# First two attention units gathered whole, and the means of v copied out of PSUM once

## The chip, the cores and the metric

The kernel runs on one core of one Trainium2 chip. The metric is the device time of one execution in microseconds: 601.21 us is the median of three runs of the kernel before (601.02 to 601.26).

## The reference, cut to what matters

Attention with a local window and block summaries, then two MLPs with their own activations. Shapes: 2 batches, 8 heads, 768 positions, head size 64; 1536 tokens of 512 in the MLPs, 2048 hidden.

```python
k_sum = k.reshape(B, H, nb, 32, D).max(axis=3)        # nb = 24
v_sum = v.reshape(B, H, nb, 32, D).mean(axis=3)
scores_l = scale * q @ k^T, where |i - j| < 16, else -1e9
scores_s = scale * q @ k_sum^T + log(32)
a = softmax(concat(scores_l, scores_s))
x = a @ concat(v, v_sum)                               # heads side by side: 1536 x 512
h = x @ w_in1;  P = a0 + a1 h + a2 h^2 + a3 h^3;  Q = 1 + |b0||h| + |b1| h^2
x = (P / (Q + 1e-6)) @ w_out1
h = x @ w_in2;  out = (h * cos(h)) @ w_out2
```

## The kernel before

The weights come as 64 bit floats. DVE puts each block together as 32 bit from its two halves (`f<-raw`, three instructions, L760 to L768), and it is then split into a high and a low part (`w`), so that a product is three matmuls of the fast 32 bit kind. Per block of 128 hidden units and 512 tokens there is a stage `h` (12 matmuls, L864), an elementwise chain (`te`, `tu`, `tf`, then `gh` and `gl`), and a stage `acc` (12 matmuls, L1106) that adds into four PSUM banks `acc0` to `acc3`. The second MLP takes its hidden blocks in pairs with seven products instead of eight (L962).

Attention has 12 units of 128 queries. A unit turns q round (`qtp`, copied to `qT`), gathers for each half of 64 queries the 96 keys of its window and the 24 block maxima into `kw` (a part of the tile `room`), and forms the scores of even and odd heads in two banks (`sp`, L626). Then come 8 score steps: DVE adds the mask and takes the maximum (`sc`, `mn`, L656), and ACT does exp with its sum (`su`, L660). The probabilities are scaled, transposed (`ptp`, copied to `pt`) and multiplied with `vw` (`avp`, L734). `vw` is one of four tiles: 96 rows of v by a load from DRAM (L722), and 24 rows of v's block means. The output goes split into `xH` and `xL`, which the first `h` reads.

At the start k of batch 0 comes in 8 loads (a pair of heads and half the positions each, into `part`), is transposed on PE into early banks (`ktp`, L463), copied to `big` and reduced to block maxima (L471). Two loads of q serve units 0 and 1. v of batch 0 comes in three loads; two positions are added (L514), and three matmuls make the means in one bank, `vmp` (L517).

The order is written out. The program first lists 3040 operations, each with its possible engines; a table (`ORDER`) then gives for every place which operation is issued next and on which engine. Each engine keeps that order, and so does SP, which issues nearly all DMAs. Waits follow from the data.

The change touches, in `v_mean0`, the copies of the means (L521 to L526); in `q_tile`, units 0 and 1 (L565 to L575); in `attn_a`, the gathering by pairs of heads (`gather`, L608 to L645); in `add_a`, where the first q is listed; and the table. At the end, `mlp_end` (L1138) does the last accumulator in two halves of 256 columns: matmuls of half one, its copy by ACT, matmuls of half two, its copy by DVE, each half with its own output DMA.

Of the kernel before, what the change touches and what calls it, by code (L numbers as in the profile page):

```python
# [11 lines left out]
F32 = mybir.dt.float32  # L12
# [9 lines left out]
QC = 1.0 + 1e-6  # L22
# [13 lines left out]
for _p, _t in (("AA", .143), ("AP", .17), ("AT", .25), ("AV", .14), ("PA", .08), ("PP", .08), ("PT", .15),  # L36
# [20 lines left out]
    "c-rk)ON?g6RsQOA-*w;jf4}<g{`)o4-P7Zq=^1+-9?wi>?7=wWB#vccTP8ROa%>aJ1|csTD`5dy#8QX>i%1qqK!CD{;t"  # L57
    "+(8B3OY4Qp5_0B|FwE*dTFk)xEbTSwz6PtN-r*KB~^+JKs5{sv+FasgQC63MdEQF^-Fy3?2?-dffr`rQ~1-$In5*agKK"
    "P57-&k`|Y{do&Zb5F~_gT=?vlcRZ+5_?~j0?E?gY!IH~l<s?;B1UKL`F0`eH%5ZANt0$7PXEnM*sR~{H}mI<6w-*>?BU"
    "w4xwmORI7%gcCzc#wUS>jW~_#U#^V`a~lC>24UnzonvA;c_U3vv1$SRovaZeVJXy^`Cy~^7auPd1?!nzJ6uv@y&<NZ+`"  # L60
    "8Mw>ED=A3eIk&ttiDaG*BVw$I@F;>PaIx39muxxd(Y=ffW@HdYHP=iglW=6rGZjrshU!{-h@eK^1J)ZxJ;>_7368{+8j"
    ";MSXm&dxp_+y1F~VQ}RqJI|~Bz0Y2LM!ga|T|Iqw?QV7VBG$@s?fO*Ct8sCCRP10l$glL5`LcI>+{@=xKAj$y<^JJ442"
    "v6sb9=~xtzMO2RSc6Kt}pU9E@x@~;ZeNX8$zF1@9S!JQQShgm`$%0FJ5&gSr!hCqgxkK#9{Hc#z7R^O2XaUca;9zPVn+"
    "p^l0R7JpZRF1n$~7S3bSkd}@AX-`(4t&1Ro~bL%Z^+<cSYxcBykb1fFvL>3L>FGhL%imPtCER!-(;%xSs*cCfa{A(X<d"
    "g8s5_j%-%-1A5L?PpzGI68Qv;K_hXeaHXH@@B+^P~KIcxqE>hE%+By@KrAu&v@`c>GHvEMcR8f{LCf~qoI10$!O&sF4<"
    "IUs)<-%jThqm#g6mLXzPn?_B;HQ1^=%R=d2j@er2!s8J4|G4El1h`^K5#e2&%n{=aR;>)6(d|JYjm%PQWO|2q~5J|7(c"
    "!GA7334h=*jEZvb&&U;IMnrlfj=_n}=lu!?z>~Lg=Mkh^Th7g^|A0qVa3X=r9J2rsyud+NIS#x?UI>q3In*8iAG^qyix"
    "ohc_#rr4?9#L!QvwP64RLw?SHQ;~<KrLb+xY%1Y=18VR)3D_&)6s3?@(qqA2|ysJ-ZDV4j_VlZ4)x2xEx22tOu`p%)3!"
# [1258 lines left out]
```

## Time and profile before

| | |
|---|---|
| median of three runs | 601.21 us (601.02 to 601.26) |
| the profiled execution | 601.26 us, of which the trace spans 599.4 |
| PE busy | 585.9 us (98%) |
| DVE busy | 548.4 us (92%) |
| ACT, POOL busy | 434.1 us (72%), 304.3 us (51%) |
| granted PE clock | full in all 40 slices |

The profile has one row of times for each engine. PE's share of 98% counts modelled ends of pipelined matmuls, so short gaps don't show in it. Where PE is not the last to be waited for is at the start, in the first 100 us, where attention and the first blocks of the MLP run side by side, and in the last few us.

### The profile page before, as it was taken

What the parts mean: (1) busy time and instruction counts of PE and PEld (TensorE: products, weight loads), DVE (VectorE), ACT (ScalarE), POOL (GpSimd) and SP (SyncE); (2) the same over time, 40 slices, a digit from 0 to 9 for tenths busy, and PEclk for the clock granted to TensorE, in tenths of its full rate; (3) what the DMA queues carried; (4) which work ended last, traced back from release to release, by engine and by line L of the source; (5) the groups of instructions that cost most, each with busy time, mean ns of one, the idle gap of its engine ahead of it and who ended that gap; (6) DMA issues with size and microseconds to landing.
All of it is one profiled execution on the core that took longest, in us unless ns stands there. A gap on an engine that the chain in (4) does not pass through costs nothing.

```text
span 599.4 us, 10933 instructions
## 1 busy us (share of the span) xinstructions
PE 585.9 (98%) x3897; PEld 501.0 (84%) x3897; DVE 548.4 (92%) x1119; ACT 434.1 (72%) x954; POOL 304.3 (51%) x303
## 2 busy tenths in 40 slices
PE   8879999999999999999999999999999999999997
PEld 7568878888888888888888888888989989998996
DVE  4999999979999999998999999999999998887874
ACT  3989999877587756876789897766767566554653
POOL 5587975247537564557577542444355423732130
PEclk9999999999999999999999999999999999999999
DMA  9897874200321313311220112123322331100104
GB/s 264 218 258 192 204 209 120 75 0 2 106 71 37 106 36 105 106 52 56 70 71 1 36 36 71 37 71 104 109 71 70 106 108 36 35 1 1 53 1 158
DMA packets 68862, 51.85 MB, mean 87 GB/s; under 512 B 37304, under 2 KB 63160, under 8 KB 68808
## 3 DMA queue, kind: packets, MB, share of 16 engines
q1 hardware_dynamic: 68664, 51.03, 29.0%
q8 instruction: 30, 0.49, 0.3%
q14 instruction: 24, 0.20, 0.1%
q10 hardware_dynamic: 144, 0.13, 0.1%
HBM read 47.71 MB, written 3.15 MB: 85 GB/s over the span
## 4 chain that ended last, share of the span: by engine, by line
PE 87%; DVE 9%; ACT 2%; DMA 1%; issue 0%; POOL 0%; SPq 0%; POOLq 0%; DVEq 0%; ACTq 0%
PE acc L1106 43%; PE h L864 22%; PE h L962 18%; DVE sc L656 2%; DMA vw<-in_v_dram 1%; PE avp L734 1%; DVE f L764 1%; DVE f L768 1%; PE ptp L687 1%; PE sp L626 1%; PE warm L356 1%; PE ktp L463 1%; DVE f L760 1%; PE vmp L542 0%; DVE big L471 0%
## 5 line engine op out<-in xcount | busy, mean ns | idle before, releaser
L1106 PE MATMUL acc<-gh,w 128*128 128x512 f32 (+1 forms) x416 | 123.1, 378 | 0.0
L1106 PE MATMUL acc<-w,gh 128*128 128x512 f32 x382 | 119.3, 394 | 0.0
L864 PE MATMUL h<-xH,w 128*128 128x512 f32 (+1 forms) x320 | 99.1, 371 | 0.1
L777 POOL TENSOR_TENSOR gl<-te,gh 128x512 fp32r<-128x512 f32 (+1 forms) x48 | 62.7, 1307 | 67.2 <-ACT gh L322 33.5
L1106 PEld LDWEIGHTS acc<-gh,w 128*128 128x128 f32 x416 | 75.3, 188 | 14.9 <-issue 1.5
L1106 PE MATMUL acc<-gl,w 128*128 128x512 f32 (+1 forms) x208 | 77.6, 373 | 0.0
L1106 PEld LDWEIGHTS acc<-w,gh 128*128 128x128 f32 x382 | 66.7, 189 | 9.4
L1106 PE MATMUL acc<-w,gl 128*128 128x512 f32 x191 | 74.3, 389 | 0.0
L1023 POOL TENSOR_TENSOR tu<-tu,tf 128x512 f32<-128x512 f32 (+1 forms) x41 | 51.4, 1255 | 41.2 <-ACT tf L1015 40.9
L777 POOL TENSOR_TENSOR w<-f,w 128x512 fp32r<-128x512 f32 x39 | 54.4, 1397 | 29.5 <-ACT w L322 15.0
L864 PEld LDWEIGHTS h<-xH,w 128*128 128x128 f32 x320 | 58.5, 188 | 10.6 <-DVE big L495 0.3
L864 PE MATMUL h<-xL,w 128*128 128x512 f32 (+1 forms) x160 | 58.9, 368 | 0.0
L864 PE MATMUL h<-big,w 128*128 128x512 f32 x216 | 52.0, 389 | 0.0
L768 DVE SCALAR_TENSOR_TENSOR f<-raw,f 128x512 int32<-128x512 int32 x64 | 48.3, 759 | 0.3
L1013 ACT ACTIVATE tu<-h,co 128x512 f32<-128x512 f32 (+1 forms) x52 | 33.9, 652 | 19.3 <-PE h L864 18.2
L764 DVE SCALAR_TENSOR_TENSOR f<-raw,f 128x512 int32<-128x512 int32 x64 | 47.3, 745 | 0.6
L864 PEld LDWEIGHTS h<-big,w 128*128 128x128 f32 x216 | 40.6, 188 | 8.4
L1106 PEld LDWEIGHTS acc<-gl,w 128*128 128x128 f32 x208 | 39.1, 188 | 7.0
L1106 PEld LDWEIGHTS acc<-w,gl 128*128 128x128 f32 x191 | 35.9, 188 | 7.9
L1057 ACT ACTIVATE tu<-te 128x512 int32<-128x512 f32 x27 | 17.1, 632 | 32.5 <-DVE te L987 32.2
L324 POOL TENSOR_SCALAR w<-f 128x512 fp32r<-128x512 f32 x28 | 20.0, 715 | 39.8 <-DVE f L768 35.1
L1033 ACT ACTIVATE h<-tf 128x512 f32<-128x512 f32 (+1 forms) x52 | 29.6, 570 | 12.0 <-DVE te L1027 10.8
(222 smaller groups left out, 1530.9 us busy)
## 6 DMA issues: line engine op xcount, KB each, us to landing
raw<-in_moe_w_in_dram SPq DMA_DIRECT2D x32, 512.0 KB, 4.6
raw<-in_moe_w_out_dram SPq DMA_DIRECT2D x32, 512.0 KB, 3.4
vw<-in_v_dram SPq DMA_DIRECT2D x24, 192.0 KB, 3.5
qk<-in_q_dram SPq DMA_DIRECT2D x10, 256.0 KB, 5.3
out_dram<-part SPq DMA_DIRECT2D x8, 256.0 KB, 2.8
part<-in_k_dram SPq DMA_DIRECT2D x8, 192.0 KB, 4.8
big<-in_v_dram SPq DMA_DIRECT2D x3, 512.0 KB, 6.7
qk<-in_k_dram SPq DMA_DIRECT2D x6, 256.0 KB, 5.4
```

The lines of the kernel that those rows point to most:

```text
L324: nc.gpsimd.tensor_scalar(out=o, in0=i, scalar1=1.0, scalar2=1.0, op0=ALU.mult, op1=ALU.mult)
L656: lambda e, pr=pr, hh=hh, sv=sv, sp=sp: nc.vector.tensor_tensor_reduce(out=sv()[:, pr, :], in0=sp.t[:, pr, :], in1=m.t, op0=ALU.add, op1=A ...
L764: lambda e: nc.vector.scalar_tensor_tensor(out=ft.t.bitcast(I32), in0=lohi()[1], scalar=-0x40000000, in1=ft.t.bitcast(I32), op0=ALU.bitwis ...
L768: lambda e: nc.vector.scalar_tensor_tensor(out=ft.t.bitcast(I32), in0=lohi()[0], scalar=29, in1=ft.t.bitcast(I32), op0=ALU.logical_shift_r ...
L777: lambda e: E[e].tensor_tensor(out=lo(), in0=x(), in1=hi().bitcast(F32), op=ALU.subtract),
L864: nc.tensor.matmul(out=h.t[:, 0:n], lhsT=lt, rhs=rt[:, kk, cs], start=(k0 == 0 and i == 0), stop=(k0 == 2 and i == 5))
L962: nc.tensor.matmul(out=bank.t[:, c], lhsT=lt, rhs=rt, start=start and i == 0, stop=stop and i == 5, skip_group_check=True)
L1013: lambda e: nc.scalar.activation(out=U(), in_=H(), func=ACTF.Square, scale=b1s))
L1023: lambda e: E[e].tensor_tensor(out=U(), in0=U(), in1=Z(), op=ALU.add))
L1033: lambda e: nc.scalar.activation(out=H(), in_=Z(), func=ACTF.Exp, scale=-1.0))
L1057: lambda e: nc.scalar.activation(out=K().bitcast(I32), in_=S_(), func=ACTF.Identity, scale=1.0 / (2.0 * math.pi)))
L1106: nc.tensor.matmul(out=dst, lhsT=lt, rhs=rt, start=(un.start and not have and i == 0), stop=(un.stop and i == 2), skip_group_check=have)
```

## The change

1. `v_mean0`: only the first `vw` tile gets the means from PSUM by an engine's copy. The other three get them from that tile by loads inside SBUF. Before, two were copied, and two loaded.
2. `q_tile` for units 0 and 1: the transposes of all four pairs of heads are one operation, and one copy of 512 columns takes the place of two of 256.
3. `attn_a` for units 0 and 1: the maxima, the windows and the score matmuls are gathered for all four pairs at once, as the other units have it; before, pair by pair.
4. `add_a`: q of unit 0 is listed after all pairs of k, not after the first.
5. A new table for 3018 operations, in place of 3040. Engines change all through the program.

```diff
 ORDER = (
-    "c-rk)ON?g6RsQOA-*w;jf4}<g{`)o4-P7Zq=^1+-9?wi>?7=wWB#vccTP8ROa%>aJ1|csTD`5dy#8QX>i%1qqK!CD{;t"
...
+    "c-rk)TaRQ{bzXa|z0dtt=Tdd5s_WWaeV^{089cXk&)CMygv{6&JYbANu%p-zWXBkgfM7uqq{twF5(^>{*)K>4cp?TOBS"
...
-        for i in range(2):
+        for i in range(1):
             P.op([("A", act(512, True)), ("V", dve(512))], [], [vp, vws[i]["m"]],
                  lambda e, i=i: cp(e, vws[i].t[WK:KW], vp.t[WK:KW]))
-        for vw in vws[2:]:
+        for vw in vws[1:]:
             P.op([("S", 0.2)], [vws[0]["m"]], [vw["m"]],
                  lambda e, vw=vw: nc.sync.dma_start(out=vw.t[WK:KW], in_=vws[0].t[WK:KW]))
...
+        if u < 2:
+            raws = [x for x, _ in q_first]
+
+            def tr(e):
+                for pr in range(NP):
+                    h0 = 2 * (pr % 2)
+                    transpose_pairs(tp.t[:, pr, :], q_first[pr // 2][1]()[:, h0:h0 + 2], 64 * u, 64)
...
-        if u < 2:
-            for i in range(2):
-                def tr(e, i=i):
-                    for x in range(2):
-                        transpose_pairs(tp.t[:, 2 * i + x, :], q_first[i][1]()[:, 2 * x:2 * x + 2], 64 * u, 64)
-
-                P.op([("T", 0.44)], [q_first[i][0]], [tp[i], dst[i]], tr)
-                P.op([("A", act(256, True)), ("V", dve(256))], [tp[i]], [dst[i]],
-                     lambda e, i=i: cp(e, dst.t[:, 2 * i:2 * i + 2], tp.t[:, 2 * i:2 * i + 2]))
...
+        P.op([("T", 0.88 if u < 2 else 0.44)], raws, [tp, dst], tr)
+        P.op([("A", act(512, True)), ("V", dve(512))], [tp], [dst], lambda e: cp(e, dst.t, tp.t))
...
-        if u < 2:
-            for y in every:
-                gather([y])
-        else:
-            gather(list(every))
...
-            fill.append((k_pair, 0, 30.0))
-            fill.append((q_tile, 0, 30.0))
-            for i in range(1, NP):
+            for i in range(NP):
                 fill.append((k_pair, i, 30.0))
```

Three places show what the table does with it. The first is DVE at its start, up to the first score steps (`sc`). Before:

```order
L327 COPY big<-ktp 128x384
L471 TENSOR_REDUCE big<-ktp 128x12 x2
L327 COPY big<-ktp 128x384 x2
L471 TENSOR_REDUCE big<-ktp 128x12 x2
L327 COPY big<-ktp 128x384
L471 TENSOR_REDUCE big<-ktp 128x12 x2
L327 COPY room<-big 128x96 x2
L327 COPY qT_301<-qtp 128x256
L656 ISA sc,mn<-sp_290,room 128x120
L656 ISA mn 128x1
L514 TENSOR_TENSOR big<-big 128x8x64
L471 TENSOR_REDUCE big<-ktp 128x12 x2
```

and after:

```order
L472 TENSOR_REDUCE big<-ktp 128x12 x8
L328 COPY qT_301<-qtp 128x512
L515 TENSOR_TENSOR big<-big 128x8x64 x2
L642 ISA sc,mn<-sp_305,room 128x120
L642 ISA mn 128x1
```

All eight copies of k are now ACT's, and DVE does two of the three additions of v, where it did one, before any score step.

The second place is SP, from the loads of the first `vw` tiles to the copies of the means inside SBUF. Before:

```order
L722 DMA vw1_391<-in_v_dram 96x8x64
L722 DMA vw0_405<-in_v_dram 96x8x64
L722 DMA vw2_419<-in_v_dram 96x8x64
L381 DMA co_104<-in_moe_b_dram 128x2
L722 DMA vw3_455<-in_v_dram 96x8x64
L526 DMA vw3_455<-vw0_405 24x512
L526 DMA vw2_419<-vw0_405 24x512
```

and after:

```order
L708 DMA vw1_326<-in_v_dram 96x8x64
L416 DMA raw_349<-in_moe_w_in_dram 128x4x128
L708 DMA vw2_370<-in_v_dram 96x8x64
L708 DMA vw0_383<-in_v_dram 96x8x64
L382 DMA co_104<-in_moe_b_dram 128x2
L416 DMA raw_404<-in_moe_w_out_dram 128x512
L527 DMA vw1_326<-vw0_383 24x512
L527 DMA vw3_430<-vw0_383 24x512
L527 DMA vw2_370<-vw0_383 24x512
```

`vw0` and `vw1` are what unit 0 reads. The means of `vw1` now come by a DMA that stands behind the coefficient load `co` and a load of weights.

The third place is PE's end, the two halves of the last accumulator (128x256) and what stands between them. Before:

```order
L1106 MATMUL acc3_6875<-w1_6329,gh_6886 128x512 x2
L1106 MATMUL acc3_6875<-w1_6329,gl_6892 128x512
L1150 MATMUL acc3_6875<-w1_6434,gh_6906 128x256 x2
L1150 MATMUL acc3_6875<-w1_6434,gl_6911 128x256
L1106 MATMUL acc2_6848<-w1_6434,gh_6906 128x512 x2
L1106 MATMUL acc2_6848<-w1_6434,gl_6911 128x512
L1150 MATMUL acc3_6875<-w1_6434,gh_6906 128x256 [waits Activation_49]
```

and after:

```order
L1092 MATMUL acc3_6865<-w1_6321,gh_6857 128x512 x2
L1092 MATMUL acc3_6865<-w1_6321,gl_6875 128x512
L1136 MATMUL acc3_6865<-w1_6452,gh_6892 128x256 x2
L1136 MATMUL acc3_6865<-w1_6452,gl_6894 128x256
L1136 MATMUL acc3_6865<-w1_6452,gh_6892 128x256 [waits Activation_49]
```

The group of another accumulator that stood between the halves has moved ahead of both.

## Rows read from the trace of the kernel before

**Rows 1.** The page: busy time by engine; the chain that ended last.
```profile
PE 585.9 (98%) x3897; PEld 501.0 (84%) x3897; DVE 548.4 (92%) x1119; ACT 434.1 (72%) x954; POOL 304.3 (51%) x303
...
PE 87%; DVE 9%; ACT 2%; DMA 1%; issue 0%; POOL 0%; SPq 0%; POOLq 0%; DVEq 0%; ACTq 0%
```
**Rows 2.** Stretches: length, PE, PEld, DVE, ACT, POOL busy; clock, DMA share, GB/s.
```profile
15.00:25.00 10.00, 8.20 (x120) 4.45 (x114) 9.65 (x48) 8.76 (x41) 5.52 (x6) 1.00 0.83 191
30.00:75.00 45.00, 40.02 (x507) 35.25 (x510) 44.79 (x156) 42.28 (x144) 37.08 (x41) 1.00 0.86 218
75.00:590.00 515.00, 514.94 (x3010) 441.84 (x3000) 480.49 (x878) 371.04 (x736) 251.00 (x220) 1.00 0.21 66
```
**Rows 3.** Timeline of PE, 5 to 13 us: start, length, instructions.
```profile
7.39 0.68 PE L432 MATMUL qtp<-ident,part 64*64 64x64 f32 x16
8.66 0.68 PE L432 MATMUL qtp<-ident,part 64*64 64x64 f32 x16 [0.59 <-ACT qT L322]
9.28 3.58 PE L463 MATMUL ktp<-ident,part 128*64 128x128 f32 x60
```
**Rows 4.** ACT and DVE groups by form, 0 to 80 us: busy, mean ns.
```profile
L322 ACT COPY big<-ktp 128x384 f32<-128x384 f32 x4 | 1.9, 480 | 6.6 <-PE ktp L463 6.6
...
L471 DVE TENSOR_REDUCE big<-ktp 128x12 f32<-128x384 f32 x8 | 4.1, 547 | 0.3 <-ACT big L322 0.3
...
L327 DVE COPY qT<-qtp 128x512 f32<-128x512 f32 x1 | 0.7, 678 | 0.0
...
L327 DVE CAST w<-f 128x512 fp32r<-128x512 f32 x1 | 0.4, 422 | 0.0
```
**Rows 5.** Instructions of L514 and L777: ns min/median/max, first and last start.
```profile
L514 POOL TENSOR_TENSOR big<-big x2: 1275/1496/1717, 14.3 to 15.6; 128x512 f32<-128x512 f32 x2
L514 DVE TENSOR_TENSOR big<-big x1: 1514/1514/1514, 14.6 to 14.6; 128x512 f32<-128x512 f32 x1
...
L777 DVE TENSOR_TENSOR w<-f,w x24: 678/685/1093, 34.4 to 543.0; 128x512 fp32r<-128x512 f32 x24
```
**Rows 6.** Timeline of DVE: unit 0's steady score steps, and unit 2's first.
```profile
17.00 0.27 DVE L656 CUSTOM_DVE_ANT_0 sc<-sp,room 128x120 f32<-128x120 f32 x1
...
24.71 0.28 DVE L656 CUSTOM_DVE_ANT_0 sc<-sp,room 128x120 f32<-128x120 f32 x1
```
**Rows 7.** Timeline of SP's queue around the copies of v's means.
```profile
17.05 4.44 SPq L381 DMA_DIRECT2D co<-in_moe_b_dram  x1
...
22.63 1.77 SPq L526 DMA_DIRECT2D vw<-vw  x2
```
**Rows 8.** Timeline, 23 to 32 us, of all engines, from the means to unit 0's product.
```profile
23.67 0.58 ACT L322 COPY vw<-vmp 24x512 f32<-24x512 f32 x1
...
25.14 1.15 PE L734 MATMUL avp<-pt,vw 120*64 120x64 f32 x30 [0.51 <-ACT pt L322]
...
27.73 0.19 PEld L734 LDWEIGHTS avp<-pt,vw 120*64 120x64 f32 x2 [0.67 <-ACT pt L322]
```
**Rows 9.** DMA issues: line, count, KB each, median us to landing.
```profile
vw<-in_v_dram SPq DMA_DIRECT2D x24, 192.0 KB, 3.5
...
out_dram<-room SPq DMA_DIRECT2D x1, 128.0 KB, 1.9
```
**Rows 10.** Timeline of the end, from half one to the last DMA.
```profile
594.23 0.28 PE L1150 MATMUL acc<-w,gl 128*128 128x256 f32 x1
...
594.35 0.63 PE L1106 MATMUL acc<-w,gh 128*128 128x512 f32 x2
594.55 0.37 ACT L322 COPY room<-acc 128x256 f32<-128x256 f32 x1 [1.12 <-PE acc L1150]
...
595.05 0.43 PE L1150 MATMUL acc<-w,gh 128*128 128x256 f32 x2
...
595.70 0.42 DVE L327 COPY room<-acc 128x256 f32<-128x256 f32 x1 [1.49 <-PE acc L1150]
596.40 0.38 SPq L1159 DMA_DIRECT2D out_dram<-room  x1
```

More of the change, by code (lines that the diff above doesn't have):

```diff
@@ L105 @@
+    "-<~lt%Y58Iwq3?oF(ZP7g@I{b=w$cjn-Q;SdT!mTQpZ~5q&2|wx6WSomT3O+OjWo#_hIUV&KpJ0+sF;69"
 )
@@ L562, in q_tile, with tr @@
                      prio=P.now - lead)
[L563 to L584 removed]
+        if u < 2:
[4 more added lines that the diff above has]
+                    transpose_pairs(tp.t[:, pr, :], q_first[pr // 2][1]()[:, h0:h0 + 2], 64 * u, 64)
+        else:
+            raws = [load([128, NH, D], F32, "qk", "qk", 3,
+                         q[b, :, 128 * t:128 * t + 128, :].rearrange("h s d -> s h d"), lambda t: t, 1.3,
+                         P.now - lead)]
+            def tr(e):
+                for pr in range(NP):
+                    nc.tensor.transpose(tp.t[:, pr, :], raws[0].t[:, 2 * pr:2 * pr + 2], ident)
+        dst = qTs[u % NQ]
+        P.op([("T", 0.88 if u < 2 else 0.44)], raws, [tp, dst], tr)
+        P.op([("A", act(512, True)), ("V", dve(512))], [tp], [dst], lambda e: cp(e, dst.t, tp.t))
         P.now += 0.44
@@ L603, in attn_a @@
         sps = [psum([128, NP, KW], f"sp{hh}") for hh in range(2)]
+        kks = {kr["k", i, y] for w in ws for i in range(w // 128, (w + WK - 1) // 128 + 1)
+               for y in range(NP)}
         kw = kws[u % NKW]
[L605 to L639 removed]
@@ L641, in attn_a, with windows @@
-        if u < 2:
-            for y in every:
-                gather([y])
-        else:
-            gather(list(every))
+        if t < NKW:
+            P.op([("P", Shared(0.6)), ("A", act(192))], [kr[x] for x in kr.subs if x[0] == "s"], [kw["s"]],
+                 lambda e: cp(e, kw.t[:, :, :, WK:KW],
+                              ks().unsqueeze(2).to_broadcast([128, NP, 2, NB])))
+        def windows(e):
+            if ws[1] - ws[0] == 64:
+                x = kk()[:, :, ws[0]:ws[0] + 128].rearrange("p n (a s) -> p n a s", a=2)
+                x = bass.AP(x.tensor, x.offset, [x.ap[0], x.ap[1], x.ap[2], [1, WK]])
+                cp(e, kw.t[:, :, :, 0:WK], x)
+            else:
+                for half in range(2):
+                    cp(e, kw.t[:, :, half, 0:WK], kk()[:, :, ws[half]:ws[half] + WK])
@@ new lines, in attn_a, with mm @@
+        n = 768
+        P.op([("P", Shared(0.85)), ("A", act(n)), ("V", dvef(n))], sorted(kks, key=id), [kw["w"]], windows)
+        def mm(e):
+            for pr in range(NP):
+                for half in range(2):
+                    for hh in range(2):
+                        p0, c0 = 64 * hh, 64 * half
+                        nc.tensor.matmul(out=sps[hh].t[c0:c0 + 64, pr, :],
+                                         lhsT=qt.t[p0:p0 + 64, pr, c0:c0 + 64],
+                                         rhs=kw.t[p0:p0 + 64, pr, half, :], start=True, stop=True)
@@ L646, in attn_a @@
+        P.op([("T", SPT)], [qt, kw["s"], kw["w"]], sps, mm)
         su = new("sm", [128, 2, NP], F32, "su", 3)
@@ L1199, in add_a @@
                 fill.append((k_tile, i, LEADK))
-        if u:
-            fill.append((q_tile, u, 30.0 if u < 2 else 8.0))
+        fill.append((q_tile, u, 30.0 if u < 2 else 8.0))
         fill.append((attn_a, u))
```

136 lines of the change are left out of this document (48 added, 88 removed).

## The prediction

> **What bounds the kernel now.** I read the shares by engine first, then the chain of work that ended last [rows 1]. PE is busy for 98% of the span, and 87% of the chain lies on it, 9% on DVE. So the end is PE's work plus what PE idles, and the change leaves PE's matmul work as it is. The next question is where PE idles, and the table by stretches says it [rows 2]: from 75 to 590 us PE is busy in 514.94 of 515.00 us, at the full granted clock. Nothing can be gained there, only lost. From 30 to 75 us it idles 45.00 - 40.02 = 4.98 us, and there DVE is busy in 44.79 of 45.00, ACT in 42.28. From 15 to 25 us it is DVE again, 9.65 of 10.00. So up to 75 us the kernel runs at DVE's pace, and an instruction saved on DVE ahead of that point is worth its time at the end; after it, it is worth nothing. The third place is the tail behind 590 us, where one chain of PE, a copy and a DMA sets the end.
>
> The sum is made against the profiled execution, 601.26 us, whose span is 599.4 (1.86 lie around it); it stands 0.05 above the median of 601.21.
>
> **Start, DVE up to unit 2's first score step.** In before, that step starts at 24.71 [rows 6]; it is my marker, since by then both kernels have done units 0 and 1's score steps. I build its time in after by hand. k comes in eight halves. PE stands at the first qtp at 7.39 with two halves done [rows 3]; in after the other six (72 matmuls) follow with no q between, at 3.58 / 60 = 0.06 each: 4.3 us, to 11.7. One copy by ACT (0.48) and one reduce by DVE (0.547) [rows 4] bring 12.7. In before PE also stood for 0.59 us until qT was copied [rows 3]; this wait goes, and q's copy of 512 columns (0.68 [rows 4]) takes its place on DVE: 13.4 to 13.6. Then come two additions of v. The same shape costs 0.685 in DVE's 24 others, but 1.514 in the one that ran beside POOL's addition [rows 5]. I take 0.685, since POOL's only addition can lie beside at most part of two: the steps begin at 15.0, and at 16.6 with the dear price.
>
> From 17.00, where 15 of unit 0's and 1's 16 steps are left, before needs 24.71 - 17.00 = 7.71 us [rows 6]. After has one step more (0.27 [rows 6]), one CAST of a weight (0.42 [rows 4]) and one gathered window copy of 128x768 on DVE. No such copy is in the trace; 1.5 times the CAST is 0.63, 1.5 times the 512 column copy out of PSUM (0.68) 1.02; I take 0.63, as both CAST and copy read SBUF. Against that, about 0.1 us of small steps go. So 7.71 + 0.27 + 0.42 + 0.63 - 0.1 = 8.9, and 15.0 + 8.9 = 23.9: **a lead of 0.8 us** for DVE. With the dear additions and the dear copy it is 25.9, 1.2 late.
>
> **The new wait for v's means.** Unit 0's product reads vw0 and vw1. Before, both were copied out of PSUM; the later by ACT, 0.58 us, ending 24.25, and the main run of products started at 25.14 [rows 8]. Now vw1's means come from vw0 by a DMA. vw0 is copied by DVE behind unit 1's last step, which by the sum above ends near 19.9. SP's queue however stands for 4.44 us in the load of `co` in before (17.05 to 21.5) [rows 7], and in after the copy stands behind that load and a load of weights. With that stall it issues at about 22.0. What it takes to land: 1.9 us is the least median in the table, for the output DMA, 3.5 that of a load of vw [rows 9]; an upper end is 5.1, since in before copies issued from 22.63 [rows 7] were read by 27.73 [rows 8]. So it lands between 23.9 and 27.1; I take the middle of the two medians, 24.7. That is 0.4 before 25.14, where DVE's lead of 0.8 alone would have put the product at 24.3. Behind the products on PE stand their copies, xH and xL on DVE, and the first `h`: when the DMA is late, DVE waits at xL. So of 0.8 us the wait leaves 0.3 to 0.5. **Term A: -0.5 us.** Its ends are -1.3 (SP doesn't stand, the copy of the means costs DVE nothing it hadn't paid before) and +2.0 (landing at 27.1).
>
> Here the Trainium skill speaks against the change: in "DMA: Bandwidth & Descriptors", section "Anatomy of one DMA — SWDGE (gpsimd) path", it puts a fixed cost of about 2.0 us on every DMA, most of it the receipt of the last write, where an engine's copy has none of it. For 48 KB its fit would give 2.1 us (an estimate from that page, made for another queue than SP's), so the means would be there at 24.1 instead of 24.7, and A would be -0.7; the trace of before shows no landing time for this copy.
>
> **30 to 75 us.** I compared DVE's instructions up to common markers (the end of each unit's output) by their durations in before: equal within 0.1 us. ACT has about 1.5 to 2 us less by 60 us, as copies move from it. As DVE stands full at 44.79 [rows 2], the relief on ACT counts only where DVE waits for ACT, which is at most the 0.21 us that DVE idles there, and PE's waits for ACT's copies. **Term C: -0.2 us**, with ends of -1.0 (half of ACT's relief) and +1.0 (POOL's additions standing where DVE waits for them).
>
> **75 to 590 us.** The table moves some 10 us of elementwise work from DVE, in part to POOL, whose additions of this shape take 1.3 to 1.7 us against DVE's 0.685 [rows 5]. POOL is busy in 251.00 of 515.00 us [rows 2], so it has room, and PE's buffers cover a late `gl` as long as it stays one block ahead. I take 0. It can't be below 0 by more than the 0.06 us that PE idles; above, each block that is late costs 0.6 to 1.0 us (the difference of the two engines).
>
> **The tail.** Before, between the two halves of the last accumulator PE does another accumulator's three matmuls (594.35 to 595.05), and under them ACT copies half one, 594.55 to 594.92; half two starts at 595.05, DVE copies it from 595.70 to 596.12, and the last DMA is issued at 596.40 [rows 10]. Half two must wait for ACT's copy of half one, as they are in one tile. After, the three matmuls stand ahead of both halves, so half one ends 0.70 later, ACT's copy ends at 595.62, and half two starts behind it with nothing of PE's between, at 595.73 instead of 595.05. Its copy ends at 596.80. The cover that hid ACT's copy is gone; what comes back is that in before the last DMA was issued 0.28 behind the copy's end, with SP busy on the other accumulator's outputs. In after those go out 0.7 earlier, and SP is free: issue at 596.83. **Term B: +0.43 us**, with ends 0 (an earlier order of copies and DMAs shortens the rest by as much) and +0.7 (SP as late as before).
>
> **Sum:** 601.26 - 0.5 - 0.2 + 0 + 0.43 = 600.99, so **601.0 us**, no change within what a measurement of this kernel can tell (0.2%, 1.2 us).
>
> **The rivals.** *Faster.* DVE's lead of 0.8 comes through whole, with SP not standing for 4.4 us in `co` (a load's stall depends on what is in the queue ahead, and three loads ahead of it have moved): A = -1.3; ACT's relief lets another -1.0 through; B stays. 601.26 - 1.3 - 1.0 + 0.43 = 599.4. For it speaks that DVE and ACT together bound PE up to 75 us, and that 22 operations are gone; against it that only waits that PE sees count. Chance 0.32, with the part between -1.2 and that.
>
> *Slower, the late means.* The copy of vw1's means lands at 27.1 rather than 24.7, since it stands in one queue behind weights and the DMA engines are busy in 83% there [rows 2]. Unit 0's product, xL and the first `h` wait for it; DVE, with its instructions in a fixed order, stands at xL. A = +1.5 to +2.0, and with B the time is 601.26 + 1.75 + 0.43 - 0.2 = 603.2. It decides from a landing at about 25.9 on. Against it: the loads just ahead are few. Chance 0.13.
>
> *Slower, the additions of v.* Both take 1.514 as the one in before: the lead turns into 1.2 late, and 601.26 + 1.2 + 0.43 - 0.2 = 602.7. In the row, one addition on DVE lay beside two on POOL; in after two lie beside one, which speaks for one dear addition at most, a lead of 0 and 601.5, within no change. The Trainium skill has a reason for the row, in "SBUF — State Buffer", section "SBUF: two separate sides": an operation of DVE with two inputs in SBUF and one of GpSimd that reads SBUF exclude one another for a whole instruction. By that rule, only the first of DVE's two could be held, by one POOL addition; 1.514 against 0.685 fits it. Chance 0.06.
>
> *Slower, POOL's share.* One to three blocks behind 75 us come late by 0.6 to 1.0 each, in a stretch where PE has no slack: 601.0 + 1.8 = 602.8. For it speaks that PE is at 100% there, so that every wait is lost time; against it POOL's 49%. Chance 0.08.
>
> **How the numbers follow.** The forecast (601.0, from 600.1 to 602.4 by its own ends) has 0.41, the faster case 0.32, the slower ones 0.13 + 0.06 + 0.08 = 0.27. The range for 8 in 10 leaves about 0.1 at each side: from 599.0, a little below the faster case, to 603.0. Chances: faster by over 0.2% 0.32, within 0.41, slower 0.27.
>
> **What would show it.** In the profile after: DVE's two additions of v at 0.69 or 1.5 us each; unit 2's first score step at 23.9 (right) or at 24.7 and later (A wrong); the main run of unit 0's product released by the DMA of vw1 at about 24.7, and how long SP stood in `co`; PE's busy time from 75 to 590 us still within 0.1 of the stretch; in the tail, half two waiting on ACT's copy for about 0.7 us and the last DMA 0.43 later against half one's block. The forecast is wrong if PE idles more than 0.6 us behind 75 us, or if PE's idle time ahead of it differs by more than 1.2 us from before.

## The result, and the profile after

The changed kernel took 608.08 us (607.03 to 609.68, four runs) against 601.24: a ratio of 1.0116 (1.0101 to 1.013), slower by 6.8 us where no change was forecast. The same kernel, run once more later (e15), took 601.06, and in twelve further runs (e16) 601.8 to 609.3, median 604.92 (1.0055, 1.0031 to 1.0079). So it has no single time, and the question becomes what decides between 601 and 609.

The first profile, of 607.86 us (span 606.1): the page's busy times and the chain that ended last, which answer to [rows 1].

```profile
PE 587.2 (97%) x3897; PEld 501.4 (83%) x3897; DVE 550.2 (91%) x1096; ACT 434.4 (72%) x951; POOL 320.9 (53%) x311
...
PE 73%; DVE 20%; issue 2%; DMA 2%; ACT 2%; SPq 0%; POOL 0%; DVEq 0%; ACTq 0%; POOLq 0%
```

DVE has 23 instructions fewer and is busy 1.8 us longer; of the chain it holds 20% where it held 9%. The stretches, with the columns of [rows 2]:

```profile
25.00:30.00 5.00, 2.38 (x39) 1.80 (x38) 3.77 (x16) 3.28 (x12) 1.53 (x3) 0.93 0.99 268
30.00:35.00 5.00, 4.33 (x43) 3.62 (x43) 3.82 (x20) 3.61 (x15) 3.14 (x3) 0.50 1.12 296
35.00:40.00 5.00, 5.00 (x62) 4.80 (x62) 4.24 (x15) 3.90 (x14) 2.47 (x5) 0.89 0.89 229
75.00:590.00 515.00, 512.44 (x3002) 437.55 (x3001) 480.80 (x862) 368.92 (x744) 273.43 (x237) 1.00 0.21 65
```

and the first two of them in the kernel before:

```profile
25.00:30.00 5.00, 4.27 (x74) 3.46 (x74) 5.00 (x21) 4.97 (x18) 3.00 (x3) 1.00 0.92 273
30.00:35.00 5.00, 3.73 (x53) 3.11 (x53) 5.00 (x28) 4.43 (x19) 3.88 (x3) 1.00 0.96 246
```

Two things stand here that before has not: from 25 to 35 us DVE, full in before, idles 2.4 us, and the granted clock goes to half (the 1.2 GHz level); and from 75 to 590 us PE idles 2.6 us where it idled 0.06.

PE's matmuls are the same in these kernels (3897 in each profile; e5 below adds 18), so one measure serves for all: the time at which PE stands, less the usual interval (0.227 us for 512 columns, and so on) of every matmul issued by then. That is what PE has lost. Against the kernel before, in us:

| profile | lost up to 150 us | from 150 to 300 | after 300 | the run's time |
|---|---|---|---|---|
| changed kernel, first | +2.1 | +4.1 | +0.7 | 607.86 |
| changed kernel, second (e15) | -0.9 | +0.3 | +0.7 | 601.06 |
| changed kernel, third (e16) | -1.0 | +5.6 | +0.7 | 606.52 |

(The column "after 300" counts PE alone; of the 0.7 the output takes back 0.25.) The start loses 2 us in one profile of three and gains 0.9 to 1.0 in two; the later part adds 0.3 or 4 to 6, and nothing between.

**The start.** The first profile's timeline, all engines, around unit 2's first step and the load of q of unit 3:

```profile
23.47 1.15 PE L720 MATMUL avp<-pt,vw 120*64 120x64 f32 x32
23.91 0.51 SPq L416 DMA_DIRECT2D qk<-in_q_dram  x1
24.12 0.28 DVE L642 CUSTOM_DVE_ANT_0 sc<-sp,room 128x120 f32<-128x120 f32 x1
...
26.43 1.15 PE L720 MATMUL avp<-pt,vw 120*64 120x64 f32 x30 [0.16 <-ACT pt L323]
...
29.12 0.43 DVE L746 TENSOR_SCALAR f<-raw 128x512 int32<-128x512 int32 x1 [1.23 <-DMA raw<-in_moe_w_in_dram]
...
29.81 1.12 PE L578 MATMUL qtp<-ident,qk 128*128 128x128 f32 x4 [2.24 <-DMA qk<-in_q_dram]
```

Unit 0's product starts at 23.47, 1.67 us before its place in [rows 8], unit 1's at 26.43. So PE had its lead here, larger than forecast. Then PE stands 2.24 us for a load, and DVE 1.23 for another: both engines had become faster than the loads. While PE stands, the granted clock falls: it is at half from 29.26 to 36.09.

**The later part.** What PE waited for from 150 to 300 us, in the first profile (us in total, times, longest); in the second profile this list is empty, as in before:

```profile
PE acc L1092 <- ACT acc L323: 0.9, 1, 0.9
PE acc L1092 <- POOL gl L763: 0.7, 1, 0.7
PE h L850 <- DVE te L1027: 0.7, 1, 0.7
PE acc L1092 <- DVE acc L328: 0.2, 1, 0.2
```

The list holds 2.5 of the 4.1 us; gaps under the modelled ends of matmuls don't show in it. Following the late `te` and `gl` back, operation by operation, against the second profile, DVE stays 3.1 us behind it from 153 to 182 us, and then falls back at single instructions, each one beside an instruction of POOL: it is 4.1 behind at 186 us, 5.3 at 213 and 6.8 at 221. The first profile there, DVE and POOL:

```profile
182.37 1.30 POOL L763 TENSOR_TENSOR gl<-te,gh 128x512 fp32r<-128x512 f32 x1 [1.60 <-DVE gh L328]
...
182.51 1.45 DVE L746 TENSOR_SCALAR f<-raw 128x512 int32<-128x512 int32 x1
...
184.86 1.30 POOL L1009 TENSOR_TENSOR tu<-tu,tf 128x512 f32<-128x512 f32 x1 [0.42 <-ACT tf L1001]
184.90 1.54 DVE L746 TENSOR_SCALAR f<-raw 128x512 int32<-128x512 int32 x1
```

and the same four instructions in the second profile:

```profile
179.29 1.29 POOL L763 TENSOR_TENSOR gl<-te,gh 128x512 fp32r<-128x512 f32 x1 [1.60 <-DVE gh L328]
...
179.43 1.44 DVE L746 TENSOR_SCALAR f<-raw 128x512 int32<-128x512 int32 x1
...
181.80 1.58 POOL L1009 TENSOR_TENSOR tu<-tu,tf 128x512 f32<-128x512 f32 x1 [0.45 <-ACT tf L1001]
181.81 0.42 DVE L746 TENSOR_SCALAR f<-raw 128x512 int32<-128x512 int32 x1
```

The second f<-raw takes 1.54 us in the one and 0.42 in the other. In the one it starts 0.04 behind POOL's addition and ends 0.28 after it; in the other they start level, and POOL's is the one that takes longer (1.58). DVE is 1.1 us later from there on, and so it meets POOL's next instructions late too. In the first profile at 211 to 219 us:

```profile
211.45 1.30 POOL L763 TENSOR_TENSOR w<-f,w 128x512 fp32r<-128x512 f32 x1 [1.46 <-ACT w L323]
211.48 1.81 DVE L763 TENSOR_TENSOR gl<-te,gh 128x512 fp32r<-128x512 f32 x1
...
214.48 1.51 DVE L746 TENSOR_SCALAR f<-raw 128x512 int32<-128x512 int32 x1
...
218.52 1.28 POOL L1009 TENSOR_TENSOR tu<-tu,tf 128x512 f32<-128x512 f32 x1 [1.32 <-ACT tf L1001]
218.62 1.75 DVE L750 SCALAR_TENSOR_TENSOR f<-raw,f 128x512 int32<-128x512 int32 x1
```

In the second profile these three instructions of DVE take 0.68, 0.84 and 0.68. From 200 to 250 us DVE is busy in 48.9 of 50 us in the first profile, so little absorbs it.

**The tail**, to be read against [rows 10]:

```profile
601.13 0.28 PE L1136 MATMUL acc<-w,gl 128*128 128x256 f32 x1
601.45 0.37 ACT L323 COPY room<-acc 128x256 f32<-128x256 f32 x1 [1.12 <-PE acc L1136]
...
601.87 0.50 PE L1136 MATMUL acc<-w,gh 128*128 128x256 f32 x2 [0.46 <-ACT room L323]
...
602.60 0.42 DVE L328 COPY room<-acc 128x256 f32<-128x256 f32 x1 [2.85 <-PE acc L1136]
603.05 0.33 SPq L1145 DMA_DIRECT2D out_dram<-room  x1
```

PE has lost 6.22 us up to 590. 603.05 less that is 596.83, 0.43 behind the 596.40 of before. The same sum gives 596.8 in the second and third profile.

### The profile page after: what moved, and what is told of

Read it like the earlier page. It is cut to its first block, busy times and chain, and to the rows that moved or that the text cites. A ratio compares the mean times of both kernels' runs of the same rounds, so it can differ in the third digit from the quotient of the medians.

```text
span 606.1 us, 10913 instructions
## 1 busy us (share of the span) xinstructions
PE 587.2 (97%) x3897; PEld 501.4 (83%) x3897; DVE 550.2 (91%) x1096; ACT 434.4 (72%) x951; POOL 320.9 (53%) x311
## 4 chain that ended last, share of the span: by engine, by line
PE 73%; DVE 20%; issue 2%; DMA 2%; ACT 2%; SPq 0%; POOL 0%; DVEq 0%; ACTq 0%; POOLq 0%
PE acc L1092 34%; PE h L948 17%; PE h L850 15%; DVE te L1027 2%; DVE te L1013 2%; DVE tu L1021 2%; DVE f L754 2%; DVE te L1011 2%; DVE h L1024 2%; DMA qk<-in_q_dram 2%; DVE f L746 2%; PE sp L627 2%; DVE f L750 2%; PE avp L720 1%; PE ptp L673 1%
## 5 line engine op out<-in xcount | busy, mean ns | idle before, releaser
L850 PE MATMUL h<-xH,w 128*128 128x512 f32 (+1 forms) x320 | 100.6, 375 | 0.6 <-DVE big L496 0.6
L763 POOL TENSOR_TENSOR gl<-te,gh 128x512 fp32r<-128x512 f32 (+1 forms) x51 | 67.4, 1321 | 45.9 <-ACT gh L323 32.9
L1009 POOL TENSOR_TENSOR tu<-tu,tf 128x512 f32<-128x512 f32 (+1 forms) x46 | 59.7, 1300 | 23.1 <-ACT tf L1001 23.0
L763 POOL TENSOR_TENSOR w<-f,w 128x512 fp32r<-128x512 f32 x39 | 56.1, 1441 | 26.7 <-ACT w L323 13.4
L754 DVE SCALAR_TENSOR_TENSOR f<-raw,f 128x512 int32<-128x512 int32 x64 | 50.0, 788 | 0.3
L750 DVE SCALAR_TENSOR_TENSOR f<-raw,f 128x512 int32<-128x512 int32 x64 | 48.1, 757 | 0.2
L1016 ACT ACTIVATE tf<-tu 128x512 f32<-128x512 f32 (+1 forms) x52 | 31.3, 602 | 17.5 <-POOL tu L1009 14.8
L325 POOL TENSOR_SCALAR gh<-te 128x512 fp32r<-128x512 f32 (+1 forms) x27 | 18.8, 695 | 45.6 <-DVE te L1055 24.5
```

The source lines that it names most:

```text
L325: nc.gpsimd.tensor_scalar(out=o, in0=i, scalar1=1.0, scalar2=1.0, op0=ALU.mult, op1=ALU.mult)
L750: lambda e: nc.vector.scalar_tensor_tensor(out=ft.t.bitcast(I32), in0=lohi()[1], scalar=-0x40000000, in1=ft.t.bitcast(I32), op0=ALU.bitwis ...
L754: lambda e: nc.vector.scalar_tensor_tensor(out=ft.t.bitcast(I32), in0=lohi()[0], scalar=29, in1=ft.t.bitcast(I32), op0=ALU.logical_shift_r ...
L763: lambda e: E[e].tensor_tensor(out=lo(), in0=x(), in1=hi().bitcast(F32), op=ALU.subtract),
L850: nc.tensor.matmul(out=h.t[:, 0:n], lhsT=lt, rhs=rt[:, kk, cs], start=(k0 == 0 and i == 0), stop=(k0 == 2 and i == 5))
L1009: lambda e: E[e].tensor_tensor(out=U(), in0=U(), in1=Z(), op=ALU.add))
```

## The experiments

Two theories at first: the start is late (q's load, the clock) and all else follows from that; or the later part of the new table loses by itself. "The later part of X" below means order and engines of X for all operations left at 150 us. Times are medians with the range of the runs; each group of runs had the kernel before beside it on the same chip, at 600.97 to 601.82.

### Which part loses

```diff
 SP, changed kernel (e1; e2 moves the load of weights up as well)
  DMA vw1<-vw0
+ DMA qk<-in_q_dram
  DMA vw3<-vw0
  DMA vw2<-vw0
  DMA vw2<-in_v_dram
  DMA raw<-in_moe_w_in_dram
- DMA qk<-in_q_dram
```

> The changed kernel with one load moved in SP's order: q of unit 3 goes right behind the first copy of v's means (to vw1), ahead of the two other copies, a load of vw and a load of weights. In the changed kernel it is issued at 23.91 and lands at 29.77, and PE waits for it 2.24 us from 27.58; the granted clock is at half from 29.26 to 36.09. Theory (the load of q is what is late next, and PE's idle time there costs the clock too): q lands before 27.6, the wait of 2.24 us is gone, the clock stays full, and the time lost up to 150 us against the kernel before falls from 2.1 us to under 0.5. If the 4.1 us lost between 200 and 260 us come from the later part of the table by itself, the time is 608.1 - 2 = 606; if they are a debt handed on from the start, 602. Rival (DVE, not q, sets the start: it waits for a load of weights until 29.12 as well): the wait moves to DVE's scores and the time stays at 607.5 to 608.

Measured: 607.15 (601.26 to 608.98). A miss for the median. Its profile was of the 601.26: no wait for q, full clock, -0.8 up to 150 us, +0.3 after.

> As the run before, with the load of weights that DVE waits for until 29.12 (1.23 us) moved up too, right behind the load of q. If DVE's wait for the weights is worth its time at the end, this is up to 1.2 us faster than the run with q alone: about 605 (later part to blame for the rest) or 601 (debt). If DVE's time there is not what bounds, no difference to the run with q alone. The copies of v's means to vw2 and vw3 stand behind 768 KB now; if they land after 26 they cost unit 1's product up to 0.8 us.

Measured: 607.98 (604.04 to 612.7); nothing gained by the weights.

```diff
 the table (e3: a = changed, b = before; e4: a = before, b = changed)
+ order up to 150 us: a
+ order and engines of what is left: b
```

> The changed kernel's order up to 150 us, and from there the order and the engines of the kernel before, as far as operations are left. If the 4.1 us lost between 200 and 260 us (and 0.7 at the end) lie in the later part of the table, the time is 601.2 + 2.1 = 603.3. If they are a debt from the start (DVE 2 us behind at 150 us in both kernels' terms), they stay, only the tail comes back: 608.1 - 0.7 = 607.4.

> The kernel before's order up to 150 us, and from there the order and the engines of the changed kernel. If the later part of the new table loses by itself: 601.2 + 4.1 + 0.7 = 606.0, and DVE's instructions beside POOL's are stretched by some 9 us more than before between 150 and 300 us. If it is a debt from the start: 601.2 + 0.7 = 601.9.

Measured: e3 602.04 (599.79 to 607.05), e4 602.38 (601.26 to 603.93). With both ends changed 608.1, with either one 602. Neither theory has room for that: the losses don't add up, so I took it that the start does something to the later part. A slow time alone doesn't tell which part lost, though: four runs of e3 took 603.1 to 607.1, with a granted clock of 0.991 to 0.994 over the run, its eight others 599.8 to 603.2 with 0.996 or more.

### The start, and what it hands on

```diff
             def tr(e):
+                for i in range(18 if u == 3 else 0):
+                    nc.tensor.transpose(tp.t[:, i % NP, :], ident, ident)
                 for pr in range(NP):
```

> The changed kernel, with 18 transposes of the identity (0.108 us each, 1.95 us) into the bank of unit 3's q, ahead of the real ones, in the place where PE waits 2.24 us for the load of q; the real ones overwrite them. The wait itself stays, but PE works in it. Theory (a part of what is lost at the start is the clock, at half from 29.26 to 36.09): the clock stays full there, and of the 2.1 us lost up to 150 us about 1 goes (what PE does from 29.8 to 36 at half pace); then the time is 607 if the later part loses its 4 us all the same, 602 to 604 if the later part loses only when the start is late. Rival (the clock costs nothing, DVE bounds there): 608, with the clock full.

Measured: 605.4 (602.4 to 609.93). The profile, of the slowest run, shows another cause of a late start, in unit 0's product:

```profile
25.59 1.76 PE L720 MATMUL avp<-pt,vw 120*64 120x64 f32 x28 [1.77 <-DMA vw<-vw]
```

This is the load inside SBUF that the first part of the change brings; here the clock fell at 25.5, in that wait and before the added work. What the clock costs by itself can't be read from a kernel whose times lie so far apart.

```diff
 the table (e6; e12 the same with v's means as in e11 and q ahead of all copies of means)
+ order up to 150 us: the changed kernel's, q early as in e1
+ order and engines of what is left: before's
```

> The start of the changed kernel with q of unit 3 loaded earlier (as in the first run), and from 150 us on the order and engines of the kernel before. Of the runs with the later part of before, those with a full clock took 599.8 to 601.9, those with less up to 607. Theory (PE's wait for q pulls the clock down, and the later part of before hands on what the start loses without adding to it): the clock stays full and the time is 599.8 to 600.8, below the kernel before. Rival (the start of the changed kernel loses in some other way): 602 or more, with a full clock.

Measured: 600.88 (599.92 to 603.17), against 601.36: ratio 1.0 (0.9985 to 1.0014). In its profile the start is 1.0 ahead and stays so to the end; over all runs it gains nothing that can be measured. No version here beats the kernel before.

```diff
 table of the changed kernel, from 150 us (e7)
- engine of each elementwise operation: as in the changed kernel
+ engine of each elementwise operation: as in the kernel before
```

> The changed kernel's order all through, but from 150 us on each elementwise operation is on the engine that it has in the kernel before: 60 leave POOL, 50 come to it. Theory (DVE's instructions are held by POOL's where they meet, and the new assignment makes them meet where DVE has no slack): fewer are held between 150 and 300 us, the 4.1 us lost there shrink to 0 to 1, time 603.5 to 604.5. Rival (the order, not the engines, is what loses): 607 to 608.

Measured: 637.61, a miss, and it settles nothing: an order is made for its engines, and 173 operations on others queue behind the wrong neighbours. PE loses 20 us from 150 to 300 and 17 after.

> The kernel of the first run once more, for a second profile. Its times lay between 601.3 and 609.0, and the profile was of the 601.3. Theory (the start's lateness varies with the loads, and the later part of the new table turns a small delay into several us where DVE's instructions meet POOL's): a run at 604 to 609 shows its loss between 180 and 260 us with a full clock there, and DVE instructions there that last 0.3 to 1.1 us more than in the quick run. Rival: the loss is at the start, before 150 us.

Measured: 609.85, +1.7 up to 150 us (the clock at half for 3.4 us from 24.6) and +5.6 from 150 to 300, its second f<-raw 0.04 behind POOL's addition and 1.54 long. So both losses, where the quick run of the same kernel had neither.

```diff
     def to_f32(raw, ft, prio):    # calls 3 to 7 only
-             lambda e: nc.vector.tensor_scalar(...)
+             lambda e: [nc.vector.tensor_scalar(...) for _ in range(2)]
```

> The kernel before, with the first instruction of five weight blocks' reassembly (0.42 us each on DVE, between 29 and 51 us) issued twice: 2.1 us more of DVE's work where DVE is full, no other change. Both theories: the start is 2.1 us later, and the later part of before hands that on as it is: 601.3 + 2.1 = 603.4 (less, if PE's wait there is not DVE's alone).

> The same 2.1 us of DVE's work put into the start of the kernel before, with the order and engines of the changed kernel from 150 us on (which alone took 602.4). Theory (the later part of the new table turns a late start into several us more): 602.4 + 2.1 + about 4 = 608 to 609, the surplus lost between 180 and 260 us, where DVE's instructions begin while POOL's run. Rival (what is lost at the start is handed on as it is, and the changed kernel's own start is what loses the rest): 604.5.

Measured: e9 605.28 (605.19 to 606.5), e10 606.0 (605.72 to 607.21). My theory of then falls: 2.1 us of DVE's work cost 4.0 in the kernel before itself, all of it by 150 us (+4.4 in its profile), and the new later part added 0.3, not 4, to a start that was 3.1 late. Why 2.1 became 4.0 is not shown in full: in e9's profile two of the five added instructions took 0.72 in place of 0.42, and the clock was at half for 6.8 us from 43.2; but three runs with a full clock took 605.2 to 605.3 all the same. In e10's profile f<-raw meets POOL's addition the good way. Lateness as such is not what decides.

```diff
-        for i in range(1):
+        for i in range(2):
             P.op([("A", act(512, True)), ...  # means of v; vw1's by ACT, ahead of q's copy of unit 2
```

> The changed kernel with its first part undone: vw1's means are copied out of PSUM by ACT again (0.58 us, ahead of the copy of q of unit 2), and two tiles get them by loads. In two slower profiles of kernels with the changed start the copy of the means to vw1 landed at 25.5 to 25.7, in the quicker ones at 23.2 to 23.5, and in one of them PE waited 1.77 us for it. Theory (this load's landing is one source of the late start): fewer late starts, median 1 to 3 us below 608.1; q's load is still late, so not below 604. Rival (q's load alone matters): 608.

Measured: 603.81 (602.31 to 605.02), 4.3 below the first timing of the changed kernel, 1.1 below the later one, neither of them run beside it. But its profile has +1.6 up to 150 us, little better than the first profile's 2.1, and +0.3 after: in this profile at least, the gain is in the meeting that goes the good way, not in the wait. Whether the first part of the change costs anything by itself stays open.

> The start of the changed kernel with both loads mended (vw1's means by ACT's copy, q of unit 3 ahead of the copies of means), and from 150 us on the later part of before. If the two loads were all that was wrong with the start, its lead comes through with a full clock: 600.0, and with less spread than the 599.9 to 603.2 of the run with q alone mended; below the kernel before by 0.2%. If PE's idle time in 14 to 22 us (1.3 to 1.5 us at a time) still pulls the clock down now and then, 600.9 as there.

Measured: 602.58 (600.88 to 604.85), worse than the run with q alone mended (600.88), against my expectation: its start is +0.3 in the profile, with PE waiting 1.9 us at unit 3's scores and the clock at half from 29.2 to 32.6.

### One meeting

In ten profiles with the new later part, the start of the second f<-raw against POOL's addition, and its length:

| f<-raw starts | its length | profiles | lost from 150 to 300 |
|---|---|---|---|
| 0.26 to 0.27 us ahead | 0.41 to 0.42 | e4, e10, e11 | +0.3 |
| 0.01 behind | 0.41 to 0.42 (POOL's 1.58) | e1, second | +0.3 |
| 0.03 to 0.27 behind | 1.51 to 1.55 | first, third, e2, e5, e8 | +4.1 to +6.8 |

So I moved one operation, and then made the meeting happen where it had not.

```diff
 one row of the changed kernel's table (e13, e17; e14 with q early as well)
- POOL TENSOR_TENSOR gl<-te,gh    # from 182.37
+ DVE  TENSOR_TENSOR gl<-te,gh
```

> The changed kernel with one operation moved from POOL to DVE: the gl that POOL starts at 182.37, beside which DVE's f<-raw from 182.51 takes 1.45 us in place of 0.42. In the four slow profiles with the new later part, a second f<-raw then starts 0.04 to 0.27 us behind POOL's addition tu<-tu,tf and takes 1.51 to 1.55 us; in the three quick ones it starts level with it or up to 0.27 us ahead and takes 0.42, and the three later meetings that cost 1.1, 0.7 and 1.1 us more in the slow ones don't happen. Theory (this meeting at 185 us decides 4 of the 6.9 us): with gl on DVE (0.69) the first f<-raw is short, the second is ahead of POOL's addition, and the loss between 180 and 260 us falls from 4.1 to under 1: 604 to 604.5. Rival (the later part meets POOL somewhere else instead; one operation decides nothing): 607 to 608.

> The same with q of unit 3 loaded earlier, as in the first run (607.2 by itself). Theory: the start's 2 us go in the runs with a full clock, the later 4 us go in all: median 601.5 to 603, best runs at 600.5. Rival: 606 to 607.

Measured: e13 602.24 (600.52 to 603.71, 12 runs), e14 601.79 (601.1 to 604.87). e13 is quicker than the 604 to 604.5 expected: in its profile the start lost nothing either. Whether one operation of 3018 gives all this back needs the changed kernel beside it:

> The changed kernel once more, for a second profile beside the first. Theory: the loss falls into the same three places: up to 150 us 1.5 to 2.5 us, between 180 and 260 us about 4 if the second f<-raw starts behind POOL's addition and under 1 if ahead, 0.4 at the end. Rival: it lies elsewhere.

> The changed kernel, timed again beside the two that follow on one chip, since one look at it gave 601.06 with the meeting at 185 us gone the good way (POOL's addition and DVE's f<-raw level, and POOL the one held). Theory (one meeting decides some 4 us, and a few tenths of a us in the start decide the meeting): two groups of times, about 601 to 603 and 606 to 610, with few between. Rival (it is a matter of degree): a spread without a gap.

> The changed kernel with the one gl on DVE, beside the changed kernel itself on the same chip. Theory: no times above 604.5; median 602 again, whatever the changed kernel does there. Rival (the chip made the difference, not the gl): the same times as the changed kernel's.

Measured: e15 601.06, e16 604.92 (601.78 to 609.25), e17 on the same chip as e16 602.09 (601.21 to 603.31, 12 runs; ratio to before 1.0007, 0.9996 to 1.0018). e16's times are four at 601.8 to 602.3, then 604.3 to 609.3: a group and a gap, though its upper part is a spread. The granted clock doesn't sort them: 606.70 with 1.000, 602.15 and 602.21 with 0.997. So one operation of 3018, on the same chip, gives back 2.8 of the 3.1 us that e16 is behind the kernel before. With gl on DVE, the two engines there (e17):

```profile
179.52 0.69 DVE L761 TENSOR_TENSOR gl<-te,gh 128x512 fp32r<-128x512 f32 x1
...
180.78 0.42 DVE L744 TENSOR_SCALAR f<-raw 128x512 int32<-128x512 int32 x1
...
181.84 0.42 DVE L744 TENSOR_SCALAR f<-raw 128x512 int32<-128x512 int32 x1
...
182.32 1.29 POOL L1007 TENSOR_TENSOR tu<-tu,tf 128x512 f32<-128x512 f32 x1 [3.48 <-ACT tf L999]
```

gl costs DVE 0.69, but the first f<-raw is 0.42 in place of 1.44, and the second is through before POOL starts. This takes both meetings at the place away and doesn't tell them apart; but the first one costs 1.44 in the quick second profile too. The next run pushes the second meeting.

```diff
     def to_f32(raw, ft, prio):    # e18: kernel e4, call 19 only, the f<-raw at 179.7
-             lambda e: nc.vector.tensor_scalar(...)
+             lambda e: [nc.vector.tensor_scalar(...) for _ in range(2)]
```

> The converse: the start of the kernel before with the later part of the new table (602.4, all 12 runs between 601.3 and 603.9, its f<-raw 0.27 us ahead of POOL's addition), and one f<-raw ahead of that place issued twice, 0.42 us more of DVE's work at 180 us and nothing else. Theory: the second f<-raw now starts behind POOL's addition, is held, and the four later meetings follow: 606 to 607 in all runs, with 4 us lost between 200 and 260 us. Rival (0.42 us is handed on as it is, or vanishes in slack): 602.4 to 602.8.

Measured: 604.91 (603.87 to 607.36; ratio 1.0056, 1.0035 to 1.0077), where e4 took 602.38 with 603.93 as its slowest (1.0021, 1.001 to 1.0032). In e4's profile, POOL and DVE at the place:

```profile
179.71 1.15 DVE L759 TENSOR_SCALAR f<-raw 128x512 int32<-128x512 int32 x1
...
181.80 0.42 DVE L759 TENSOR_SCALAR f<-raw 128x512 int32<-128x512 int32 x1
...
182.07 1.30 POOL L1022 TENSOR_TENSOR tu<-tu,tf 128x512 f32<-128x512 f32 x1 [0.72 <-ACT tf L1014]
```

and in e18's, of a 606.54:

```profile
179.52 1.91 DVE L763 TENSOR_SCALAR f<-raw 128x512 int32<-128x512 int32 x2
...
181.87 1.44 POOL L1026 TENSOR_TENSOR tu<-tu,tf 128x512 f32<-128x512 f32 x1 [0.72 <-ACT tf L1018]
...
182.07 1.52 DVE L763 TENSOR_SCALAR f<-raw 128x512 int32<-128x512 int32 x1
```

The added instruction, beside POOL as well, lengthens the first f<-raw from 1.15 to 1.91; the second then starts 0.20 behind POOL's addition and takes 1.52. In this profile PE loses 5.8 us from 150 to 300, in e4's 0.3. The median moved by 2.5 (by 1.9, when each is taken against the kernel before on its own chip), less than the 4 expected, and two of the six runs are no slower than e4's slowest: the direction is clear of noise, the size is not the same in every run.

## Why the prediction was wrong

**The lead of the start (terms A and C, together -0.7)** fits two profiles of the changed kernel in its number, -0.9 and -1.0, and not the first, +2.1. The steps in it, from the first profile: DVE's additions of v took 0.68 and 0.97 (0.685 taken), with 1.23 us of waiting for a load of v between them that the sum hasn't; the scores began at 15.4 (15.0), and unit 2's first step came at 24.12 (23.9), a lead of 0.59 where 0.8 was forecast. SP didn't stand 4.44 us in `co`, so the copies of the means were issued 1.7 us before the 22.0 that I took:

```profile
17.59 1.00 SPq L382 DMA_DIRECT2D co<-in_moe_b_dram  x1
...
20.31 2.40 SPq L527 DMA_DIRECT2D vw<-vw  x3
```

PE had no wait for them there. In the second and third profile it had, 0.71 and 0.98 us, and the main run of unit 0's product is released by the load at 24.35 and 24.44, near the 24.7 forecast. From the second:

```profile
20.14 2.41 SPq L527 DMA_DIRECT2D vw<-vw  x3
...
24.35 1.04 PE L720 MATMUL avp<-pt,vw 120*64 120x64 f32 x28 [0.71 <-DMA vw<-vw]
```

The wait is the one that the prediction named, but its time is right by luck: the copy went out some 2 us earlier than taken, and PE could go on 4.2 and 4.5 us after the issue in place of 2.7. The rival "the late means" is what e5's profile shows, 1.77 us of waiting: it happens in some executions.

**What I left out of the start** is the load of q of unit 3. I had looked for what is late next at the means alone. The row for the second candidate was at hand in the trace of before, where q's transposes start just as PE comes free:

```profile
28.22 1.15 PE L734 MATMUL avp<-pt,vw 120*64 120x64 f32 x30 [0.16 <-ACT pt L322]
29.36 0.66 PE L581 MATMUL qtp<-ident,qk 128*128 128x128 f32 x4
```

So a lead of PE's there can turn into a wait, unless the load moves up too. In the first profile the load was issued 1.1 us earlier than in before, and PE got it at 29.8, 0.45 later than it had used it in before; in the second and third PE waited 0.71 and 0.9 us for it and still kept its lead. In the first profile this wait and the clock stand beside the +2.1; their shares are not told apart.

**The later part (a term of 0)** is the step that failed; PE's idle time behind 75 us came out at 2.6 us, over the 0.6 that the prediction named as its limit. I priced POOL's share at the difference of the two engines' lengths, 0.6 to 1.0 us for a late block, and gave it a chance of 0.08 with 1.8 us at most. The price was in a row that I read for the additions of v alone: 1.514 in place of 0.685 beside POOL [rows 5]. The same hold on f<-raw, gl and the rest takes up to 1.1 us of DVE's own time at a meeting, and DVE, at 480 of 515 us in [rows 2], is full in stretches: from 200 to 250 us 49.65 of 50.00 in before. One meeting lost makes the next ones late: 4.1 us in the first profile, 5.6 in the third. Here the rule that the prediction quoted holds far beyond the place where I used it. In the Trainium skill, "SBUF — State Buffer", section "SBUF: two separate sides", whichever starts first, an operation of DVE that uses both of its ports or has two inputs in SBUF, or one of GpSimd that reads SBUF, has the shared ports for its whole length. The rows agree, both ways: DVE's 1.54 when it is second by 0.04, POOL's 1.58 in place of 1.30 when the two start level. The prediction had used the rule for two inputs alone; f<-raw has one, and is held as well.

**The tail (term B, +0.43)** was right: 596.83 forecast for the last issue, 596.83 measured with the lost time taken off. Its mechanism is there too: half two waits for ACT's copy of half one. The profile shows 0.46 us of that wait, where about 0.7 was named.

So 601.0 is near what the kernel takes when the loads are nearly in time and the meeting goes the good way: 601.06 in the second profile, with 0.2 more gained at the start than forecast and 0.3 lost in the later part. One of the kernel's cases was taken for the only one. Not settled: how much of the first profile's 2.1 us is the clock (in e14's profile it was at half for 3.4 us from 22.6, and PE was 0.8 ahead at 150 us all the same), what the first part of the change costs by itself, how the meeting went in the runs without a profile, and why four runs of four took 607 or more and the next twelve went both ways.

## What to carry to other kernels

Where an engine is full, look in the trace for its instructions that last longer than others of their form, and at what ran beside them: that row shows what moving more work to the neighbour can cost wherever the two meet. A table whose engines meet within hundredths of a us can have more than one time, as here; look at several profiles before a difference is put down to an edit. And when a stage is made faster, list every load that its consumers read, and ask of each when it lands, not only of the one that was changed.

## What the runs showed of the hardware

Over the first profile, f<-raw (one input, 32 bit integers) takes 0.40 to 0.43 us in the 31 places where no instruction of POOL runs beside it; in 19 where it starts inside a TENSOR_TENSOR of POOL the median is 0.59 and the longest 1.54. Of these 19, 15 end 0.28 to 0.29 us behind the end of POOL's instruction, however long that leaves them waiting; the other four start near its end and take their 0.41 to 0.42. The 60 `h<-tu,h` that start inside such an instruction have a median of 0.695, as the others do (0.69); one of their operands is in PSUM. So not every pair of instructions holds one another, but certain forms do.

The landing of a load differs between profiles by more than an engine's copy does. DVE's copy of the means takes 0.70 us in the three profiles of the changed kernel. The load of the means to vw1, issued at 20.0 in one profile (e5) and at 20.3 in another (e17), had landed at 25.5 and 23.0, with the last of its pieces 4.2 and 1.4 us behind the first.

In the first profile PE idled for 2.24 us up to 29.81, and the granted clock was 0.50 from 30 to 35 us (the 1.2 GHz level). The half level lasted 6.8 us there, as in e2's and e9's profiles, and 3.4 us in those of e5, e8, e12, e14 and e17.
